# Pieces of an FFT placed by tables between the matmuls of an MLP, with the PSUM banks written down

## The chip, the cores and the metric

The kernel runs on one core of one Trainium2 chip. The metric is the device time of one execution in microseconds, and the kernel before has a median of 809.14 us over 3 runs (807.16 to 809.75). The engines are called as in the profile: PE (TensorE matmuls), PEld (TensorE weight loads), DVE (VectorE), ACT (ScalarE), POOL (GpSimd) and SP (SyncE, here only a queue that issues DMAs).

## What is computed

```python
X = np.fft.rfft(x, axis=1)                    # x: 8 batches, 3008 rows, 256 columns, float32
y = np.fft.irfft(X * (filt_r + 1j * filt_i)[None], n=3008, axis=1)
h = y.reshape(8 * 3008, 256) @ w_in           # 24064 x 2048
g = np.maximum(h, 0) + alpha * np.minimum(h, 0)
out = g @ w_out                               # 24064 x 256, float32
```

Each of the eight batches is filtered along its rows in the frequency domain; all 24,064 filtered rows then go through a two-layer MLP with a leaky activation.

## The kernel before

**The MLP.** The loop at the end (L489 to L500) walks over 48 blocks of 512 or 384 filtered rows, and each block has 16 **steps**, 768 in all. A step does `up(j)` for the present block: two matmuls at L414 into a PSUM tile `hps`. In every odd step the pair of `hps` banks is full, and ACT copies it to SBUF (`gtb`, L420), after which DVE works the activation out in three instructions (two at L423, one at L424). The step also does `down` for the block before: three or four matmuls at L433 into `op`, which ACT copies out every eighth step (L438) and SP stores (L396, two or three DMAs each time). Two batches make twelve blocks, so 96 steps go by while one batch's rows pass. There are two `hps` buffers, two `op` buffers and three `osb` buffers.

**The FFT.** A batch of 3008 = 47 x 64 rows is transformed in four kinds of **pieces**, each of which takes one bank of a two-bank pool, `psF`:

- A (16 pieces, L158): one matmul (L164) on the rows `xs`, evicted by ACT to `asb`. After each four pieces SP saves `asb` to DRAM (`save_a`, L167), and when all four parts are there, SP reads them back turned into `at` with four DMAs of 384 KB (`turn_a`, L171). This is the first turned array.
- B (12, L180): two matmuls (L184) on `at`. Two DVE instructions read the bank (L188 to `ww`, L189 to `uu`), so that the bank is held until the second has ended. POOL then issues two DMAs that swap the halves of `ww` into `sw` (L191).
- S (12, L194): DVE adds `sw` to `uu`. It needs no bank.
- C (12, L199): two matmuls (L209) on `uu`, evicted by ACT to `v`. After each three pieces SP writes `v` to DRAM (`turn_c`, L212, four DMAs), and after the last three it waits for these writes and reads everything back into `zt` with four DMAs (L224). This is the second turned array.
- D (16, L226): four small matmuls (L231) on `zt`, evicted by ACT to `yT`, which the MLP's `up` reads.

`at`, `asb`, `v` and `zt` have one buffer each; `uu` has four, `ww` and `sw` three; `xs` has four, which POOL loads (L125) for the next batch.

**What sets the order.** The schedule is manual: every engine runs its instructions in the order in which the program issues them, and a plan (a dictionary from step to pieces, L442) says which pieces are issued ahead of `up` and `down` of which step. Batches 0 to 2 have plans of their own. For a batch b from 3 to 7, with p = 96 (b - 1), the plan before (L483 to L485 with L447 to L468) is regular, in steps counted from p:

| pieces | steps from p, before |
|---|---|
| A 0 to 15 | -68, then about every 2.4 steps, to -32; saves in the step of every fourth |
| `turn_a` | -27 |
| loads of the next batch's `xs` | 6, 10, 16, 20 |
| B 0 to 11 | 5, 9, 15, 19, 25, 29, 35, 39, 45, 49, 55, 59 |
| S | 8 steps behind its B |
| C | 12 steps behind its B; `turn_c` one step behind every third, the last with `zt` at 72 |
| D 0 to 15 | 91, 92, 93, 94, 95, then every second step to 117 |

Since 96 steps lie between two batches, B and C of a batch fall together with the A pieces of the next one and the D pieces of the one before. A piece that gets a bank whose earlier piece hasn't been evicted makes PE wait, and with it everything behind it in PE's order. The pool of two banks chooses the bank of each piece when the program is built. In the built program it takes the two banks in turn, but for 30 places out of 439 where one piece gets the bank of the piece just before it.

Of the kernel before, what the change touches and what calls it, by code (L numbers as in the profile page):

```python
# [11 lines left out]
FP32 = mybir.dt.float32  # L12
# [6 lines left out]
NB = 8  # L19
DFF = 2048  # L20
NH = 32
AF = mybir.ActivationFunctionType
OP = mybir.AluOpType

# [40 lines left out]
def kernel(  # L65
# [10 lines left out]
    nc = tc.nc  # L76
# [16 lines left out]
    p_osb = ctx.enter_context(tc.tile_pool(name="p_osb", bufs=3))  # L93
    psH = ctx.enter_context(tc.tile_pool(name="psH", bufs=2, space=bass.MemoryType.PSUM))
    psO = ctx.enter_context(tc.tile_pool(name="psO", bufs=2, space=bass.MemoryType.PSUM))
    psF = ctx.enter_context(tc.tile_pool(name="psF", bufs=2, space=bass.MemoryType.PSUM))
    dram = ctx.enter_context(tc.tile_pool(name="dram", bufs=1, space=bass.MemoryType.DRAM))
    a_dram = dram.tile([NB, 96, NH, D], FP16, name="a_dram")
    v_dram = dram.tile([NB, 96, NH, D], FP16, name="v_dram")
    ctx.enter_context(tc.manual_schedule())  # L100
# [20 lines left out]
    def xrow(b, h, c):  # L121
        return bass.AP(tensor=x.tensor, offset=x.offset + (b * NFFT + NH * h + 8 * c) * D,
                       ap=[[N2 * D, N1], [1, 8 * D]])

    def load_x(b, c):  # L125
        xs = p_x.tile([2 * N1, 8 * D], FP16, name="xs")
        for h in range(2):
            nc.gpsimd.dma_start(out=xs[h * N1 : h * N1 + N1], in_=xrow(b, h, c))  # L128
        return xs

    def load_filt(dst, pbase, src, ka, kb):
# [7 lines left out]
            in_=bass.AP(tensor=src.tensor, offset=src.offset + (N1 - ka) * D,  # L139
                        ap=[[47 * D, 32], [-D, n], [1, D]]))  # L140

    def bank(wide=False):
        if wide:
            return psH.tile([128, 2, 512], FP32, name="hps")[:, 0]
        return psF.tile([128, 512], FP32, name="psF")


    class Fft:
# [5 lines left out]
        def start_a(self):  # L154
            self.asb = p_fft.tile([96, NH, D], FP16, name="asb")
            self.at = p_fft.tile([128, NK1, D], FP16, name="at")

        def piece_a(self, i, evict, wide=False):  # L158
            if i == 0:
                self.start_a()  # L160
            xs = xc[(self.b, i // 4)]
            ps = bank(wide)
            o = (i % 4) * 512
            nc.tensor.matmul(ps[0:96], wf1_s, xs[:, o : o + 512], start=True, stop=True)  # L164
            evict(self.asb[:, 2 * i : 2 * i + 2].rearrange("p a d -> p (a d)"), ps[0:96])
# [5 lines left out]
        def turn_a(self, eng, ka=0, kb=NK1):  # L171
            for h in range(2):
                for c in range(2):
                    r = h * 48 + c * NK1
                    q = c * 64 + NH * h
                    eng.dma_start(
                        out=self.at[q : q + NH, ka:kb],
                        in_=a_dram[self.b, r + ka : r + kb].rearrange("k s d -> s k d"))

        def piece_b(self, kp):  # L180
            px = bank().rearrange("p (k d) -> p k d", k=2)
            for kh in range(2):
                k1 = 2 * kp + kh
                nc.tensor.matmul(px[:, kh], twf_s[:, k1], self.at[:, k1], start=True, stop=True)  # L184
            uu = p_uw.tile([128, 2, D], FP16, name="uu", bufs=4)
            ww = p_uw.tile([128, 2, D], FP16, name="ww")
            sw = p_uw.tile([128, 2, D], FP16, name="sw")
            nc.vector.tensor_mul(ww, px, filts_s[:, 2 * kp : 2 * kp + 2])  # L188
            nc.vector.tensor_mul(uu, px, filt_s[:, 2 * kp : 2 * kp + 2])  # L189
            for o in (0, 64):  # L190
                nc.gpsimd.dma_start(out=sw[o : o + 64], in_=ww[64 - o : 128 - o])  # L191
            self.uw[kp] = uu, sw
# [6 lines left out]
        def piece_c(self, kp, evict, pv=None):  # L199
            if kp == 0:  # L200
                self.v = p_fft.tile([128, NK1, D], FP16, name="v")
                self.zt = p_fft.tile([96, NH, D], FP16, name="zt")
            us = self.uw.pop(kp)
            if pv is None:
                pv = bank().rearrange("p (k d) -> p k d", k=2)
            for kh in range(2):
                k1 = 2 * kp + kh
                for u in us:
                    nc.tensor.matmul(pv[:, kh], twi_s[:, k1], u[:, kh], start=u is us[0], stop=u is us[-1])  # L209
            evict(self.v[:, 2 * kp : 2 * kp + 2], pv)  # L210
# [26 lines left out]
    def on_act(o, i):  # L237
        nc.scalar.activation(o, i, AF.Copy)  # L238

# [75 lines left out]
    xc = {(0, c): load_x(0, c) for c in range(4)}  # L315
# [88 lines left out]
    class Block:  # L404
# [4 lines left out]
        def up(self, j):  # L409
# [6 lines left out]
            if j % 2 == 1:  # L416
                g = gtb[:, turn[0] % 17]
                turn[0] += 1
                m = p_m.tile([128, 2, 512], FP16, name="m")
                nc.scalar.activation(g[:, :, 0:tn], self.hps[:, :, 0:tn], AF.Copy)  # L420
                for i in range(2):
# [5 lines left out]
        def down(self, q):  # L427
            n = self.tn // 128
            for w in range(n * q, n * (q + 1)):
# [5 lines left out]
                if k == 15 and (si % 2 == 1 or si == n - 1):  # L435
                    m = si % 2 + 1
                    osb = p_osb.tile([128, 2, D], FP32, name="osb")
                    nc.scalar.activation(osb[:, 0:m], self.op[:, 0:m], AF.Copy)  # L438
                    for lane in range(m):
# [4 lines left out]
    def put(step, fn, *args):  # L444
        plan.setdefault(step, []).append((fn, args))

    def plan_fft(b, a0, ga, ta, b0, gap, add, lag, d0, quarters, x_at):  # L447
        f = Fft(b)
        for i in range(16):
            put(int(a0 + ga * i), f.piece_a, i, on_act)  # L450
        for c in range(4):
            put(int(a0 + ga * (4 * c + 3)), f.save_a, c)
            if b + 1 < NB:
                put(x_at[c],
                    lambda b=b, c=c: xc.update({(b + 1, c): load_x(b + 1, c)}))
        for q in range(quarters):
            w = NK1 // quarters
            put(ta, f.turn_a, nc.sync, w * q, w * q + w)
        bs = [b0 + (2 * int(gap * kp / 2) if add else int(gap * kp)) for kp in range(12)]
        for kp in range(12):  # L460
            put(bs[kp], f.piece_b, kp)
            if add:
                put(bs[kp] + add, f.piece_s, kp)
            put(bs[kp] + lag, f.piece_c, kp, on_act)
        for q in range(4):
            put(bs[3 * q + 2] + lag + 1, f.turn_c, q)
        for i in range(16):
            put(d0 + min(i, 4) + 2 * max(i - 4, 0), f.piece_d, i, on_act)  # L468
# [13 lines left out]
    plan_fft(2, 66, 2, 97, 109, 4.5, 8, 12, 187, 4, (110, 114, 118, 122))  # L482
    for b in range(3, NB):  # L483
        p = 96 * (b - 1)
        plan_fft(b, p - 68, 2.4, p - 27, p + 5, 5, 8, 12, p + 91, 1, (p + 6, p + 10, p + 16, p + 20))  # L485

    prev = None
    step = 0
# [43 lines left out]
```

## Time and profile before

| | |
|---|---|
| time, median of 3 runs | 809.14 us (807.16 to 809.75) |
| span of the profiled execution, first to last instruction | 805.5 us |
| own time of the profiled execution | not given beside its span |
| first `up` of step 0 | 37.58 us into the span |
| granted TensorE clock, mean | 0.999 |
| busy: DVE, ACT, POOL | 647.0, 599.1, 140.4 us |
| moved by DMA | 100.59 MB, 125 GB/s on the mean |

Busy times of the profile are sums of the durations of instructions. A matmul's recorded duration holds its passage through the array, so that two matmuls in a row overlap in the record; what PE really gives is seen in the distance from one start to the next. "Idle before" of a group is the time in which its engine did nothing ahead of it, and the name behind the arrow is what ended the wait. All stretches are counted in us from the span's start.

### The profile page before, as it was taken

How to read it: one execution, taken by the hardware profiler on the slowest of the kernel's cores; microseconds unless marked ns; L12 is line 12 of the kernel's file. 1: busy time of each engine (PE TensorE's matmuls, PEld its weight loads, DVE VectorE, ACT ScalarE, POOL GpSimd, SP SyncE). 2: the span in 40 equal slices, each digit the busy share in tenths (PEclk: the TensorE clock that was granted, in tenths of full speed). 3: DMA queues.
4: the chain of work that ended last, by engine and by line, in shares of the span. 5: the costliest groups of instructions: out<-in, count | busy, mean ns of one | idle time of the engine just before them, and what ended most of it. 6: DMA issues, size and time to landing. Idle time of an engine off the chain costs nothing.

```text
span 805.5 us, 16163 instructions
## 1 busy us (share of the span) xinstructions
PE 781.5 (97%) x5980; PEld 538.6 (67%) x5980; DVE 647.0 (80%) x1449; ACT 599.1 (74%) x836; POOL 140.4 (17%) x269
## 2 busy tenths in 40 slices
PE   6999999999999999999999999999999999999997
PEld 5756666666666666766667666766666666776665
DVE  4797985899879897798878888798877999777773
ACT  3788677878778777877868877787877867696663
POOL 7410330232004220131102321032200222000000
PEclk9999999999999999999999999999999999999999
DMA  9977457674756446574484543854465233511111
GB/s 187 199 146 207 106 133 176 185 153 120 166 135 125 110 128 149 138 142 112 112 200 99 113 126 104 211 110 112 114 160 141 53 97 85 134 40 34 41 40 53
DMA packets 94247, 100.59 MB, mean 125 GB/s; under 512 B 11320, under 2 KB 81992, under 8 KB 94040
## 3 DMA queue, kind: packets, MB, share of 16 engines
q1 hardware_dynamic: 79512, 68.80, 32.3%
q0 software_dynamic: 14656, 30.75, 20.1%
q8 instruction: 47, 0.77, 0.4%
q14 instruction: 32, 0.26, 0.1%
HBM read 56.26 MB, written 46.66 MB: 128 GB/s over the span
## 4 chain that ended last, share of the span: by engine, by line
PE 74%; DVE 12%; ACT 7%; issue 3%; DMA 3%; SPq 1%; POOL 0%; ACTq 0%; DVEq 0%; POOLq 0%
PE op L433 32%; PE hps L414 31%; ACT gtb L420 4%; DVE m L423 4%; DVE gtb L424 3%; PE psF L209 3%; PE psF L164 2%; DVE ww L188 2%; DVE uu L189 2%; PE psF L231 2%; PE psF L184 1%; ACT asb L238 1%; DMA xs<-in_x_dram 1%; DMA v_dram<-v 1%; ACT osb L438 1%
## 5 line engine op out<-in xcount | busy, mean ns | idle before, releaser
L420 ACT ACTIVATE gtb<-hps 128x1024 f16<-128x1024 f32 (+1 forms) x384 | 385.4, 1004 | 111.2 <-PE hps L414 110.6
L433 PE MATMUL op<-wout_s,gtb 128*128 128x256 f16 x3008 | 451.1, 272 | 0.6 <-DVE gtb L424 0.6
L414 PE MATMUL hps<-yT,win_s 128*128 128x512 f16 (+1 forms) x1536 | 449.1, 374 | 0.4 <-ACT gtb L420 0.2
L433 PEld LDWEIGHTS <-gtb 128*128 128x128 f16 x3008 | 293.3, 98 | 189.5 <-DVE gtb L424 0.9
L423 DVE TENSOR_SCALAR m<-gtb,alm_s 128x512 f16<-128x512 f16 (+1 forms) x768 | 237.7, 351 | 108.1 <-ACT gtb L420 107.3
L424 DVE TENSOR_TENSOR gtb<-gtb,m 128x1024 f16<-128x1024 f16 (+1 forms) x384 | 261.6, 681 | 24.3 <-PE hps L414 0.5
L191 POOL DMA_DIRECT2D sw<-ww x168 | 87.7, 527 | 503.1 <-DVE ww L188 494.1
L414 PEld LDWEIGHTS <-win_s 128*128 128x128 f16 x1536 | 146.1, 98 | 31.1 <-issue 3.1
L238 ACT ACTIVATE yT<-psF 128x376 f16<-128x376 f32 x120 | 58.2, 485 | 25.4 <-PE psF L231 25.1
L238 ACT ACTIVATE asb<-psF 96x512 f16<-96x512 f32 x112 | 66.1, 591 | 12.4 <-PE psF L164 12.0
L238 ACT ACTIVATE v<-psF 128x512 f16<-128x512 f32 x84 | 50.2, 597 | 29.3 <-PE psF L209 28.9
L438 ACT ACTIVATE osb<-op 128x512 f32<-128x512 f32 x96 | 56.3, 586 | 6.1 <-issue 3.2
L188 DVE TENSOR_TENSOR ww<-psF,filts_s 128x512 f16<-128x512 f32 x84 | 57.4, 684 | 0.1
L189 DVE TENSOR_TENSOR uu<-psF,filt_s 128x512 f16<-128x512 f32 x84 | 57.2, 682 | 0.0
L164 PE MATMUL psF<-xs,wf_s 94*96 94x512 f16 x112 | 43.1, 385 | 1.7 <-ACT v L238 1.0
L231 PE MATMUL psF<-wi_s,zt 96*128 96x94 f16 x504 | 41.9, 204 | 2.5 <-DMA zt<-v_dram 1.6
L231 PEld LDWEIGHTS <-zt 96*128 96x128 f16 x512 | 35.4, 97 | 7.3 <-DMA zt<-v_dram 1.9
L128 POOL DMA_DIRECT2D xs<-in_x_dram x64 | 34.8, 555 | 25.6 <-PE psF L164 13.3
L209 PE MATMUL psF<-uu,twi_s 128*128 128x256 f16 x168 | 33.7, 274 | 4.9 <-DVE uu L189 4.5
L184 PE MATMUL psF<-at,twf_s 128*128 128x256 f16 x168 | 32.1, 272 | 0.2
L196 DVE TENSOR_TENSOR uu<-uu,sw 128x512 f16<-128x512 f16 x72 | 30.1, 418 | 0.0
L209 PEld LDWEIGHTS <-twi_s 128*128 128x128 f16 x192 | 16.7, 98 | 12.8 <-DVE uu L189 10.2
(57 smaller groups left out, 191.3 us busy)
## 6 DMA issues: line engine op xcount, KB each, us to landing
out_dram<-osb SPq DMA_DIRECT2D x128, 128.0 KB
xs<-in_x_dram POOLq DMA_DIRECT2D x64, 188.0 KB, 4.4
a_dram<-asb SPq DMA_DIRECT2D x28, 384.0 KB
sw<-ww POOLq DMA_DIRECT2D x168, 64.0 KB, 2.1
v_dram<-v SPq DMA_DIRECT2D x112, 96.0 KB
zt<-v_dram SPq DMA_DIRECT2D x28, 384.0 KB
at<-a_dram SPq DMA_DIRECT2D x20, 384.0 KB
at<-a_dram SPq DMA_DIRECT2D x32, 96.0 KB
```

The costliest lines, as they stand in the source:

```text
L188: nc.vector.tensor_mul(ww, px, filts_s[:, 2 * kp : 2 * kp + 2])
L189: nc.vector.tensor_mul(uu, px, filt_s[:, 2 * kp : 2 * kp + 2])
L191: nc.gpsimd.dma_start(out=sw[o : o + 64], in_=ww[64 - o : 128 - o])
L209: nc.tensor.matmul(pv[:, kh], twi_s[:, k1], u[:, kh], start=u is us[0], stop=u is us[-1])
L231: nc.tensor.matmul(ps[:, m], self.zt[:, 8 * g + 4 * mh + m, dh * 128 : dh * 128 + 128], wi3_s, start=True, stop=True)
L238: nc.scalar.activation(o, i, AF.Copy)
L414: nc.tensor.matmul(self.hps[:, j % 2, 0:tn], win_s[:, kt, j * 128 : (j + 1) * 128], yT[:, kt, self.t0 : self.t0 + tn], start=(kt == 0), st ...
L420: nc.scalar.activation(g[:, :, 0:tn], self.hps[:, :, 0:tn], AF.Copy)
L423: nc.vector.tensor_scalar(m[:, i, 0:tn], g[:, i, 0:tn], 0.0, a, OP.min, OP.mult)
L424: nc.vector.tensor_add(g[:, :, 0:tn], g[:, :, 0:tn], m[:, :, 0:tn])
L433: nc.tensor.matmul(self.op[:, si % 2], self.gts[k][:, 128 * si : 128 * si + 128], wout_s[:, k], start=(k == 0), stop=(k == 15))
L438: nc.scalar.activation(osb[:, 0:m], self.op[:, 0:m], AF.Copy)
```

## The change

The plan of batches 3 to 7 is replaced by five tables of steps, and the two banks of `psF` become two pools of one bank, with a string of 440 digits that says which of the two each piece takes, in the order of the calls. Of 439 neighbours in that string 50 have the same digit. The string also covers batches 0 to 2, whose plan is as before; its digits agree with what the pool chose up to step 70, and differ in part from there on.

In steps from p, the new plan of batches 4 to 7 is:

| pieces | steps from p, after |
|---|---|
| A 0 to 15 | -84, -82, -74, -69, -67, -61, -59, -58, -55, -53, -52, -50, -47, -44, -41, -40; saves one step behind every fourth |
| `turn_a` | -36 |
| loads of the next `xs` | 6, 10, 16, 20 |
| B | -22, -16, -12, 1, 7, 16, 23, 29, 38, 45, 51, 56 |
| S | -11, -4, -2, 11, 26, 32, 35, 41, 48, 52, 65, 67 |
| C | -1, 9, 20, 27, 34, 36, 42, 50, 54, 66, 70, 70; `turn_c` as before, the last with `zt` at 71 |
| D | 89, 90, 90, 92, 93, 94, 96, 99, 101, 101, 103, 110, 114, 121, 127, 129 |

Batch 3 keeps the old steps for A (with `turn_a` at -28), has its first three B at -12, -10 and -8 and its first S at -6, and follows the tables otherwise. The instructions themselves, their sizes and the number of DMAs are the same.

```diff
+BANKS = (
+    "010101010101010101010101010101001011100011011010100100100101010101010101010101010101010101010101"
...
+STEPS_A = (-84, -82, -74, -69, -67, -61, -59, -58, -55, -53, -52, -50, -47, -44, -41, -40)
+STEPS_B = (-22, -16, -12, 1, 7, 16, 23, 29, 38, 45, 51, 56)
+STEPS_S = (-11, -4, -2, 11, 26, 32, 35, 41, 48, 52, 65, 67)
+STEPS_C = (-1, 9, 20, 27, 34, 36, 42, 50, 54, 66, 70, 70)
+STEPS_D = (89, 90, 90, 92, 93, 94, 96, 99, 101, 101, 103, 110, 114, 121, 127, 129)
...
-    psF = ctx.enter_context(tc.tile_pool(name="psF", bufs=2, space=bass.MemoryType.PSUM))
+    psF = [ctx.enter_context(tc.tile_pool(name=f"psF{i}", bufs=1, space=bass.MemoryType.PSUM)) for i in range(2)]
...
+    order = iter(BANKS)
...
-        return psF.tile([128, 512], FP32, name="psF")
+        return psF[int(next(order))].tile([128, 512], FP32, name="psF")
...
-        plan_fft(b, p - 68, 2.4, p - 27, p + 5, 5, 8, 12, p + 91, 1, (p + 6, p + 10, p + 16, p + 20))
+        f = Fft(b)
+        steps_a = STEPS_A if b > 3 else [int(2.4 * i) - 68 for i in range(16)]
+        steps_b = STEPS_B if b > 3 else [max(st, 2 * kp - 12) for kp, st in enumerate(STEPS_B)]
+        for i in range(16):
+            put(p + steps_a[i], f.piece_a, i, on_act)
+            if i % 4 == 3:
+                put(p + steps_a[i] + 1, f.save_a, i // 4)
+        if b + 1 < NB:
+            for c in range(4):
+                put(p + (6, 10, 16, 20)[c], lambda b=b, c=c: xc.update({(b + 1, c): load_x(b + 1, c)}))
+        put(p + steps_a[15] + 4, f.turn_a, nc.sync)
+        for kp in range(12):
+            put(p + steps_b[kp], f.piece_b, kp)
+            put(p + max(STEPS_S[kp], steps_b[kp] + 6), f.piece_s, kp)
+            put(p + STEPS_C[kp], f.piece_c, kp, on_act)
+            if kp % 3 == 2:
+                put(p + STEPS_C[kp] + 1, f.turn_c, kp // 3)
+        for i in range(16):
+            put(p + STEPS_D[i], f.piece_d, i, on_act)
```

More of the change, by code (lines that the diff above doesn't have):

```diff
@@ L21 @@
 NH = 32
+BANKS = (
+    "010101010101010101010101010101001011100011011010100100100101010101010101010101010101010101010101"
+    "010101010101010101010010101010101010110101010011001011101010010101011001010101010101010110101011"
+    "001010110101010101010010010101010101010010101101010100110101010010101010101011011010101010101011"
+    "010100101010110010101011010101010101001001010101010101001010110101010011010101001010101010101101"
+    "10101010101010110101010101010101010101011010101010010101"
+)
+STEPS_A = (-84, -82, -74, -69, -67, -61, -59, -58, -55, -53, -52, -50, -47, -44, -41, -40)
[3 more added lines that the diff above has]
+STEPS_D = (89, 90, 90, 92, 93, 94, 96, 99, 101, 101, 103, 110, 114, 121, 127, 129)
 AF = mybir.ActivationFunctionType
```

## The prediction

> **What bounds the kernel now.** First the head of the page: span, busy shares, then the groups of the two MLP matmuls.
>
> ```profile
> span 805.5 us, 16163 instructions
> PE 781.5 (97%) x5980; PEld 538.6 (67%) x5980; DVE 647.0 (80%) x1449; ACT 599.1 (74%) x836; POOL 140.4 (17%) x269
> L433 PE MATMUL op<-wout_s,gtb 128*128 128x256 f16 x3008 | 451.1, 272 | 0.6 <-DVE gtb L424 0.6
> L414 PE MATMUL hps<-yT,win_s 128*128 128x512 f16 (+1 forms) x1536 | 449.1, 374 | 0.4 <-ACT gtb L420 0.2
> ```
>
> PE is the engine that is nearly always busy, and its two big groups hardly wait. But 451.1 + 449.1 is more than the span: recorded matmuls overlap, so 97% is no measure of what is left. What PE gives is read from starts, in the timeline of PE inside batch 4 (start, length, line):
>
> ```profile
> 355.36 0.60 PE L433 MATMUL op<-wout_s,gtb 128*128 128x256 f16 x4
> 355.80 0.38 PE L184 MATMUL psF<-at,twf_s 128*128 128x256 f16 x2
> 356.02 0.59 PE L414 MATMUL hps<-yT,win_s 128*128 128x512 f16 x2
> 356.45 0.60 PE L433 MATMUL op<-wout_s,gtb 128*128 128x256 f16 x4
> ...
> 357.75 0.38 PE L209 MATMUL psF<-uu,twi_s 128*128 128x256 f16 x2
> ...
> 358.84 0.38 PE L164 MATMUL psF<-xs,wf_s 94*96 94x512 f16 x1
> ...
> 359.93 0.38 PE L184 MATMUL psF<-at,twf_s 128*128 128x256 f16 x2
> ...
> 361.67 0.60 PE L433 MATMUL op<-wout_s,gtb 128*128 128x256 f16 x4
> 362.44 0.39 PE L209 MATMUL psF<-uu,twi_s 128*128 128x256 f16 x2 [0.18 <-DVE uu L189]
> ```
>
> Four `down` matmuls take 0.44 us from start to start (355.36 to 355.80), a B or C piece 0.22 (355.80 to 356.02), two `up` matmuls 0.43 (356.02 to 356.45). A step without pieces is 0.87 us, one with a piece about 1.09. At 361.67 the four `down` should have let C go at 362.11; it went at 362.44, 0.33 us late, though the idle time shown is only 0.18. What ended the wait is B's second eviction on DVE:
>
> ```profile
> 357.61 0.68 DVE L189 TENSOR_TENSOR uu<-psF,filt_s 128x512 f16<-128x512 f32 x1
> ...
> 360.50 0.69 DVE L424 TENSOR_TENSOR gtb<-gtb,m 128x1024 f16<-128x1024 f16 x1
> 361.10 0.68 DVE L188 TENSOR_TENSOR ww<-psF,filts_s 128x512 f16<-128x512 f32 x1
> 361.70 0.68 DVE L189 TENSOR_TENSOR uu<-psF,filt_s 128x512 f16<-128x512 f32 x1
> ```
>
> B went to PE at 359.93, and its bank came free at 361.70 + 0.68 = 362.38, after 2.45 us: the MLP's addition stands ahead of it on DVE. C takes that bank two steps behind B, after some 2.0 us. The B of 355.80 was free at 358.29; its bank went to the A of 358.84, three steps behind, which did not wait. So **two steps are too few and three are enough**. Now the waits of PE and of its weight loads from 236 to 648 us, which is from B of batch 3 to the last of these events (who waited for whom, us in total, times, longest):
>
> ```profile
> PE psF L209 <- DVE uu L189: 4.2, 14, 0.8
> PEld L209 <- DVE uu L189: 9.4, 22, 0.9
> PEld L164 <- DVE uu L189: 3.5, 12, 0.3
> ```
>
> The first row is the only one that this stretch has for PE, so nothing else holds it there. The loads give the count: 22 + 12 = 34 delays. In the built program, exactly 34 of the 60 B pieces of batches 3 to 7 are followed at two steps' distance by a piece in the same bank: eight a batch from 3 to 6, two in batch 7.
>
> **The change part by part.**
>
> *The 34 delays go.* With the new tables and digits the next user of a B's bank comes at two steps once, at three 4 times, and at four or more 55 times. The loads' idle time, 9.4 + 3.5 = 12.9 us, is the upper end. A load that isn't held up is done ahead, under a matmul of 0.11 us (0.44 / 4), so up to 34 x 0.11 = 3.7 us of it is no loss: the lower end is 9.2. Taking the delays singly from starts, as 0.33 above, gives 0.15 to 0.93 each, 10.3 in all, and that I take: **-10.3 us**. Nothing that PE did in these delays is lost, and what is late next is DVE and ACT, by two stretches of about 96 steps, in batches 4 and 6 (length, busy of PE, PEld, DVE, ACT, POOL):
>
> ```profile
> 332.00:428.00 96.00, 94.52 (x690) 63.45 (x689) 80.16 (x180) 75.01 (x105) 16.84 (x32) 1.00 0.56 131
> ...
> 523.00:619.00 96.00, 94.52 (x689) 63.43 (x688) 80.17 (x180) 75.00 (x105) 16.85 (x32) 1.00 0.55 131
> ```
>
> After 2.5 us less a batch, DVE has 80 us of work in 93, so it does not become the bound. The twelve B are also spread over 78 steps instead of 54.
>
> *Batches 1 and 2.* Their steps stay and the digits differ a little. One C (step 151) no longer takes the bank of the B two steps ahead, an A (step 72) now does; and in batch 3 one C (step 201) still does. With 0.4 gained and 0.1 + 0.3 lost, all sizes out of the 34, this is 0; ends -0.5 and +0.9.
>
> *Banks behind ACT.* In batches 3 to 7 a bank that ACT evicts is used again after one step 16 times, before never. Before, such cases stand in batches 1 and 2, and mostly cost nothing; the worst is the B below, one step behind an A in its bank. It should have started 0.11 us after the last C matmul and came after 0.39:
>
> ```profile
> 116.17 0.27 PE L209 MATMUL psF<-sw,twi_s 128*128 128x256 f16 x1
> 116.56 0.38 PE L184 MATMUL psF<-at,twf_s 128*128 128x256 f16 x2
> ```
>
> So 0 to 16 x 0.28 = 4.5 us. I take 0.3, since the densest new place, five pieces for ACT in steps p + 34 to 38, is 5 x 0.6 + 2 x 1.0 = 5.0 us of ACT (the pieces' and `gtb`'s mean durations, rows below) against 5 x 0.87 + 6 x 0.22 = 5.7 us of PE.
>
> ```profile
> L420 ACT ACTIVATE gtb<-hps 128x1024 f16<-128x1024 f32 (+1 forms) x384 | 385.4, 1004 | 111.2 <-PE hps L414 110.6
> L238 ACT ACTIVATE asb<-psF 96x512 f16<-96x512 f32 x112 | 66.1, 591 | 12.4 <-PE psF L164 12.0
> ```
>
> *The first turned array.* This is the step that loses its cover. From a batch's last A to its first B there were 37 steps; now there are 18, from p - 40 to p - 22: 18 x 0.87 and four C or B pieces at 0.22 are 16.5 us. The last A of batch 4 stands in PE's timeline, and SP's goes on from it (stores, save, turned read, stores, `v`, `zt`):
>
> ```profile
> 303.81 0.38 PE L164 MATMUL psF<-xs,wf_s 94*96 94x512 f16 x1
> ```
>
> ```profile
> 305.11 2.21 SPq L396 DMA_DIRECT2D out_dram<-osb  x3
> 307.42 0.38 SPq L169 DMA_DIRECT2D a_dram<-asb  x1
> 310.40 2.10 SPq L176 DMA_DIRECT2D at<-a_dram  x4
> 312.77 2.12 SPq L396 DMA_DIRECT2D out_dram<-osb  x2
> 314.93 2.11 SPq L218 DMA_DIRECT2D v_dram<-v  x4
> 321.13 1.72 SPq L224 DMA_DIRECT2D zt<-v_dram  x4
> ```
>
> The page's size of one of the four, and a stretch under them, with DMA share and GB/s at its end:
>
> ```profile
> at<-a_dram SPq DMA_DIRECT2D x20, 384.0 KB
> ```
>
> ```profile
> 313.00:316.00 3.00, 3.00 (x23) 2.02 (x22) 2.30 (x6) 1.96 (x2) 0.00 (x0) 1.00 1.19 221
> ```
>
> The turned read is issued 6.6 us behind the A; the three stores ahead of it stay there after the change, with the four writes of an earlier `turn_c` (2.1 us) ahead of these. Its 4 x 384 KB and the two stores, 1.8 MB, at the last row's 221 GB/s are an estimated 8.3 us, 8.8 with the slow start: in all 15.4 us of 16.5. So about 1 us is to spare in each of batches 4 to 7, and none if SP is a little later. I take 0.1 us a batch, 0.4 in all; ends 0 and 4 x 1.5 (the four writes in front with nothing hiding them, less the spare, and some contention). That the `zt` read now stands eleven steps behind the turned read, before three, gains nothing by itself: no row of PE waits for either in the stretch above.
>
> *The next x rows.* POOL loads them at p + 6, and the first A that needs them moves from p + 28 to p + 12. On POOL only the swaps of one B (now at p + 1) stand ahead. A B of PE with a load behind it as now, POOL's issues, and the page's medians from issue to landing:
>
> ```profile
> 335.70 0.38 PE L184 MATMUL psF<-at,twf_s 128*128 128x256 f16 x2
> ```
>
> ```profile
> 338.01 1.03 POOL L191 DMA_DIRECT2D sw<-ww  x2 [36.38 <-DVE ww L188]
> 339.03 1.05 POOL L128 DMA_DIRECT2D xs<-in_x_dram  x2
> ```
>
> ```profile
> xs<-in_x_dram POOLq DMA_DIRECT2D x64, 188.0 KB, 4.4
> ...
> sw<-ww POOLq DMA_DIRECT2D x168, 64.0 KB, 2.1
> ```
>
> That is 3.3 + 0.5 + 4.4 = 8.2 us behind the B, and eleven steps are 9.2 us or more, even in the short block, whose steps are 0.76 (0.43 x 384/512 + 0.44): 8.4 and some 0.8 for pieces. I take 0.2 us for a slow landing, ends 0 and 3.
>
> *What stays free.* S stands at least 6 steps, 5.2 us, behind its B, whose second swap is issued after 2.8 and lands in 2.1; if S waits, it holds DVE, which has room. Against D, `zt` loses one step of lead (18 instead of 19), and gains that SP no longer issues the turned read just ahead of it. The last C comes 3 steps behind its S instead of 4, of which the addition needs about two. Loads, saves and issues keep their number.
>
> **Sum.** -10.3 + 0 + 0.3 + 0.4 + 0.2 = -9.4 us, so the span goes from 805.5 to 796.1. The profile gives no own time beside its span; the runs' median, 809.14, lies 3.6 above it, and I leave that as it is: **799.7 us**.
>
> **The rivals.**
>
> *ACT's banks take over (partial gain).* If the 16 short reuses cost the full 0.28 us, 4.2 us come back: 804. For it: 50 neighbours share a bank instead of 30. Against it: 30 did so before without one PE wait for ACT in the stretch above. The Trainium skill's page "Perfetto Trace Analysis", section "Matmuls", speaks for this rival: independent groups should rotate through different banks, and the change rotates less; the trace's waits do not bear that out so far, because who evicts, and how late, decided.
>
> *The turned read comes too late (slower).* If it lands later than 16.5 us behind the last A, PE stands before B 0 in batches 4 to 7, in order, with nothing to pass it. It eats the gain at 9.4 / 4 = 2.4 us of lateness, and from 3.0 the kernel is slower by more than a measurement can tell. Were the read served at half the rate (110 GB/s, 16 us instead of 8.3), it would be late by 6.6: 4 x 6.6 - 9.8 = +17, 826 us. For it: the spare of only 1 us. Against it: the `v` writes and `zt` that competed move away.
>
> *Nothing comes of it.* PE is shown at 97%, and if that were its limit, or if DVE's lateness only moved to another wait, the time would stay at 809. Against it: the starts show 34 dated gaps, and DVE has a sixth of its time free. On the first half the Trainium skill, "Perfetto Trace Analysis", section "Identifying the Most-Contended Engine", says that matmul busy share is no good measure since matmuls overlap; the two MLP groups, 900 us in a span of 805.5, agree.
>
> **How the numbers follow.** Forecast, 797 to 802: 0.72. Short reuse or a late landing of about 1 us, 802 to 806.5: 0.16. Nothing: 0.05, at 806.7 to 811.6. Slower: 0.07. A measurement of this kernel tells about 0.3% (2.4 us) from no change. So faster 0.88, same 0.05, slower 0.07. The range is 796.5 to 804.5: below it lies only the loads' full idle time (12.9 instead of 10.3), above it the upper ends of two costs together.
>
> **What would show it.** Right: no wait of PE or its loads for `uu` L189 from batch 3 on but one, 96 steps in about 93 us where the stretches show 95 to 96, DVE and ACT as busy as before. Wrong: waits of PE for `at` or `xs` DMAs ahead of L184 or L164, waits for ACT's `asb`, `v` or `yT` ahead of `psF` matmuls, or of L433 for `gtb`.

## The result, and the profile after

The changed kernel takes **798.04 us** (median of 4 runs, 796.51 to 799.77), beside 808.15 us for the kernel before on the same chip (806.38 to 809.75, 4 runs). The ratio is 0.9879, with a 95% interval of 0.9858 to 0.9901: about 10 us faster, where 9.4 us were forecast. The profiled execution took 796.51 us itself, its span is 794.6 us, and its granted clock is 0.999 as before.

The head of the page after, with the groups of the two MLP matmuls, of `op` (L447, before L433), of C (L223, before L209) and of B (L198, before L184). The lines quoted here stand 14 lower in the kernel after than in the one before:

```profile
span 794.6 us, 16129 instructions
PE 776.0 (98%) x5980; PEld 540.0 (68%) x5980; DVE 645.2 (81%) x1449; ACT 596.8 (75%) x836; POOL 140.7 (18%) x269
PE 86%; DMA 6%; ACT 3%; DVE 2%; SPq 1%; issue 1%; POOL 0%; ACTq 0%; DVEq 0%; POOLq 0%
L447 PE MATMUL op<-wout_s,gtb 128*128 128x256 f16 x3008 | 451.1, 272 | 0.6 <-DVE gtb L438 0.6
L223 PE MATMUL psF<-uu,twi_s 128*128 128x256 f16 x168 | 32.6, 273 | 0.2
L198 PE MATMUL psF<-at,twf_s 128*128 128x256 f16 x168 | 32.1, 272 | 0.5 <-DMA at<-a_dram 0.5
```

The same 5980 matmuls run, and the busy times of DVE and ACT are within 3 us of before. The third row is the chain of work followed back from the last instruction, as shares of the span by engine. On the page of before, that row and the group of C read:

```profile
PE 74%; DVE 12%; ACT 7%; issue 3%; DMA 3%; SPq 1%; POOL 0%; ACTq 0%; DVEq 0%; POOLq 0%
L209 PE MATMUL psF<-uu,twi_s 128*128 128x256 f16 x168 | 33.7, 274 | 4.9 <-DVE uu L189 4.5
```

So DVE's share of that chain falls from 12% to 2%, and the wait of C for `uu` is gone.

Now all the waits of PE and of its weight loads after, from 236 to 760 us (who waited for whom, us in total, times, longest), in the place of the 34 of before:

```profile
PEld L198 <- issue: 1.0, 2, 0.5
PE psF L198 <- DMA at<-a_dram: 0.5, 2, 0.3
PEld L223 <- DVE uu L203: 0.2, 1, 0.2
```

One load still waits for `uu`, which is the C at step 201 that was named. The new row is the turned array `at`, twice. A stretch of 93 us after (length, busy of PE, PEld, DVE, ACT, POOL) holds as many matmuls as 96 us before (690 and 689 in the rows of the prediction):

```profile
410.00:503.00 93.00, 93.00 (x694) 64.23 (x693) 78.55 (x177) 73.51 (x103) 16.84 (x32) 1.00 0.56 135
```

For what follows, the span is cut at the first `up` matmul of every 96th step in PE's timeline. "Loop" is from the first `up` of step 0 to that of step 767. The stretch ahead of step 0, which the change does not touch, takes between 37.6 and 41.3 us in the profiled executions, so loops are compared and not spans. A delay "from starts" is, as in the prediction, the distance between two starts on PE less what it is where nothing waits.

| us | 0-95 | 96-191 | 192-287 | 288-383 | 384-479 | 480-575 | 576-671 | 672-767 | loop |
|---|---|---|---|---|---|---|---|---|---|
| before | 103.63 | 94.81 | 95.38 | 96.01 | 95.38 | 96.01 | 90.20 | 82.62 | 754.04 |
| after | 102.91 | 95.30 | 94.16 | 93.09 | 93.13 | 93.43 | 88.73 | 82.27 | 743.03 |
| C one step later | 103.82 | 94.80 | 93.78 | 93.75 | 93.78 | 93.75 | 89.68 | 82.62 | 745.99 |
| C one step earlier | 103.64 | 94.81 | 97.75 | 98.38 | 97.74 | 98.46 | 90.04 | 82.62 | 763.44 |
| tables, pool's banks | 103.84 | 96.39 | 94.04 | 93.31 | 93.13 | 93.37 | 88.74 | 82.27 | 745.09 |
| digits, old steps | 103.35 | 94.80 | 96.38 | 97.02 | 96.39 | 97.11 | 90.20 | 82.62 | 757.86 |
| turned read later | 103.96 | 100.19 | 99.47 | 97.55 | 97.98 | 97.35 | 88.74 | 82.27 | 767.51 |
| B 0 later | 103.89 | 95.30 | 93.73 | 93.09 | 93.13 | 93.09 | 88.73 | 82.28 | 743.23 |
| four edits | 104.78 | 97.12 | 93.73 | 93.09 | 93.13 | 93.09 | 88.74 | 82.27 | 745.94 |

The last seven rows are the experiments below. Each ratio that they give is to the kernel before.

### The profile page after: what moved, and what is told of

The parts are those of the page before. It is cut to its first block, busy times and chain, and to the rows that moved or that the text cites. A ratio compares the mean times of both kernels' runs of the same rounds, so it can differ in the third digit from the quotient of the medians.

```text
span 794.6 us, 16129 instructions
## 1 busy us (share of the span) xinstructions
PE 776.0 (98%) x5980; PEld 540.0 (68%) x5980; DVE 645.2 (81%) x1449; ACT 596.8 (75%) x836; POOL 140.7 (18%) x269
## 4 chain that ended last, share of the span: by engine, by line
PE 86%; DMA 6%; ACT 3%; DVE 2%; SPq 1%; issue 1%; POOL 0%; ACTq 0%; DVEq 0%; POOLq 0%
PE op L447 37%; PE hps L428 37%; PE psF L178 3%; PE psF L245 3%; PE psF L223 2%; PE psF L198 2%; ACT gtb L434 2%; DMA at<-a_dram 2%; DMA a_dram<-asb 1%; DMA filt_s<-in_filt_i_dram 1%; DMA xs<-in_x_dram 1%; ACT asb L252 1%; SPq L410 1%; PE hps L295 1%; PE psF L324 1%
## 5 line engine op out<-in xcount | busy, mean ns | idle before, releaser
L447 PE MATMUL op<-wout_s,gtb 128*128 128x256 f16 x3008 | 451.1, 272 | 0.6 <-DVE gtb L438 0.6
L447 PEld LDWEIGHTS <-gtb 128*128 128x128 f16 x3008 | 293.3, 98 | 189.5 <-DVE gtb L438 0.9
L245 PE MATMUL psF<-wi_s,zt 96*128 96x94 f16 x504 | 40.3, 204 | 1.9 <-DMA zt<-v_dram 1.1
L223 PE MATMUL psF<-uu,twi_s 128*128 128x256 f16 x168 | 32.6, 273 | 0.2
L198 PE MATMUL psF<-at,twf_s 128*128 128x256 f16 x168 | 32.1, 272 | 0.5 <-DMA at<-a_dram 0.5
L223 PEld LDWEIGHTS <-twi_s 128*128 128x128 f16 x192 | 18.4, 98 | 3.7 <-DMA sw<-ww 0.8
```

What stands on the lines that cost most here:

```text
L245: nc.tensor.matmul(ps[:, m], self.zt[:, 8 * g + 4 * mh + m, dh * 128 : dh * 128 + 128], wi3_s, start=True, stop=True)
L447: nc.tensor.matmul(self.op[:, si % 2], self.gts[k][:, 128 * si : 128 * si + 128], wout_s[:, k], start=(k == 0), stop=(k == 15))
```

## The experiments

The theory to test is that of the prediction: PE lost its time where a piece took the bank of a B, evicted late by DVE, two steps behind it, and distance is what cures that. The rivals are that the written banks do it, or that PE is at its limit anyway.

**C one step later, nothing else.** In the kernel before, C stands 13 steps behind its B:

```diff
-        plan_fft(b, p - 68, 2.4, p - 27, p + 5, 5, 8, 12, p + 91, 1, (p + 6, p + 10, p + 16, p + 20))
+        plan_fft(b, p - 68, 2.4, p - 27, p + 5, 5, 8, 13, p + 91, 1, (p + 6, p + 10, p + 16, p + 20))
```

> The plan of before with one number changed: C comes 13 steps behind its B instead of 12, so that the next user of a B's bank is never two steps behind it (42 times three, 18 times more, read from the built program). If the distance behind B is the whole cause, the 34 delays go and this lands beside the changed kernel: 8.5 to 10.3 us below before, 798 to 800. In the short blocks three steps may be too few, which would leave up to 1.5 us. If the gain needs the tables (B spread over 78 steps, reads held apart, digits), it stays within 3 us of before: 805 or more.

Measured: 799.45 us (799.18 to 801.03, 4 runs), ratio 0.9896, interval 0.9865 to 0.9927. One digit gives 8.05 of the 11.01 us that the loop gained. The waits of PE and of its weight loads from 236 to 760 us are these:

```profile
PEld L414 <- issue: 2.2, 4, 0.5
PE psF L164 <- ACT v L238: 1.6, 4, 0.4
PEld L209 <- DVE uu L189: 0.4, 2, 0.2
```

Of the waits for `uu`, two short ones of weight loads are left. What is new is four A pieces that wait for ACT. One of them, on PE and then on ACT:

```profile
378.99 0.38 PE L209 MATMUL psF<-uu,twi_s 128*128 128x256 f16 x2
...
380.08 0.38 PE L184 MATMUL psF<-at,twf_s 128*128 128x256 f16 x2
380.85 0.38 PE L164 MATMUL psF<-xs,wf_s 94*96 94x512 f16 x1 [0.39 <-ACT v L238]
```

```profile
378.81 1.01 ACT L420 ACTIVATE gtb<-hps 128x1024 f16<-128x1024 f32 x1
379.72 0.59 ACT L438 ACTIVATE osb<-op 128x512 f32<-128x512 f32 x1
380.20 0.60 ACT L238 ACTIVATE v<-psF 128x512 f16<-128x512 f32 x1
```

The C of 378.99 has its bank free only at 380.80, since `gtb` and the output copy `osb` stand ahead of `v` on ACT. The A, one step behind, should have come at 380.30 and comes 0.55 late; the four cost 2.2 us. So ACT too can hold a bank for 1.8 us; DVE held B's for 2.4.

**C one step earlier.** The same digit, 11 in place of 12:

> The plan of before with C 11 steps behind its B: 12 users of a B's bank come one step behind it and 22 two. A bank is held 2.3 to 2.9 us and a step is 0.9 to 1.1, so a distance of one costs about 1.4 us and a distance of two 0.3: 12 x 1.4 + 22 x 0.3 = 23 us of delays instead of 10.3, so about 13 us slower than before, 818 to 824. If the distance does not matter, the same as before.

Measured: 819.51 us (2 runs), ratio 1.0140, interval 1.0093 to 1.0188. The waits from 236 to 760 us:

```profile
PEld L164 <- DVE uu L189: 18.7, 24, 1.4
PE psF L164 <- DVE uu L189: 12.1, 12, 1.1
PEld L231 <- DVE uu L189: 4.6, 10, 1.1
PE psF L231 <- DVE uu L189: 1.5, 2, 0.8
```

The same engine waits for the same eviction, up to 1.4 us at a time: twelve B pieces are now followed at one step's distance and 22 at two. A cause that can be turned down by a step and up by a step is shown. The loop's last stretch, which has no B, is the same 82.62 in all three.

**The tables without the written banks.** The kernel after, with one pool of two banks:

```diff
-    psF = [ctx.enter_context(tc.tile_pool(name=f"psF{i}", bufs=1, space=bass.MemoryType.PSUM)) for i in range(2)]
+    psF = ctx.enter_context(tc.tile_pool(name="psF", bufs=2, space=bass.MemoryType.PSUM))
...
-        return psF[int(next(order))].tile([128, 512], FP32, name="psF")
+        return psF.tile([128, 512], FP32, name="psF")
```

> The changed kernel with the five tables of steps but the pool's own choice of banks (one pool of two banks, no digits). In the built program the distances behind B are nearly the same (two steps once, three 4 times, four or more 55 times), and 14 reuses come one step behind an eviction by ACT. Theory: the steps do it, the digits nothing: within 0.5 us of the changed kernel, 797.5 to 799. If the written digits carry a part, 800 or more.

Measured: 799.10 us (798.09 to 800.11, 4 runs), ratio 0.9890, interval 0.9853 to 0.9928; its interval overlaps that of the kernel after almost wholly. It lies 0.1 us above the 797.5 to 799 that were expected and below the 800 of the other theory, so the time alone settles nothing; the stretches do. From step 192 on the six stretches sum to 544.86 us, after to 544.81. There the digits do nothing. What they save lies in steps 96 to 191: 1.09 us, of which 0.70 is one D that takes a B's bank:

```profile
233.72 0.34 PE L245 MATMUL psF<-wi_s,zt 96*128 96x94 f16 x4 [0.53 <-DVE uu L203]
```

The 0.93 us more in steps 0 to 95 are longer waits for the DMAs of `sw` (+0.6) and `zt` (+0.3) of batch 1, which no bank decides and which differ from execution to execution.

**Written banks without the tables.** The kernel before with its own steps, two pools and a string chosen for these steps, so that 22 pieces instead of 34 come two steps behind a B, and 12 come one step behind an A, whose bank ACT evicts:

```diff
-    psF = ctx.enter_context(tc.tile_pool(name="psF", bufs=2, space=bass.MemoryType.PSUM))
+    psF = [ctx.enter_context(tc.tile_pool(name=f"psF{i}", bufs=1, space=bass.MemoryType.PSUM)) for i in range(2)]
...
-        return psF.tile([128, 512], FP32, name="psF")
+        return psF[int(next(order))].tile([128, 512], FP32, name="psF")
```

> The kernel before with its own steps; only the choice of the psF bank is written down, by digits chosen for these steps (two pools of one bank in place of one pool of two). A string cannot free every B bank at these steps: pieces that take their bank two steps behind a B fall from 34 to 22, 16 take it three steps behind, and 12 pieces newly take a bank one step behind an eviction by ACT. Theory one (the distance behind B is the cause, and it is the tables that make the distance): the 12 delays that go, at 0.30 each by the kernel before, are worth 3.6 us, less up to 12 x 0.1 for the ACT banks; so 803 to 806 beside 807.7, some 22 delays in the records ahead of matmuls of psF behind uu evictions. Theory two (the written banks are the change, the tables only go with them): 798 to 800. Theory three (digits bring nothing): 807 to 808.5.

Measured: **812.51 us** (811.41 to 814.28, 4 runs), ratio 1.0063, interval 1.0041 to 1.0085. All three expectations missed: it is slower than before. The waits from 236 to 760 us (C is L218 here, A L173, `asb` L247):

```profile
PEld L218 <- DVE uu L198: 8.2, 18, 1.0
PEld L218 <- issue: 6.8, 12, 0.7
PE psF L218 <- DVE uu L198: 3.7, 11, 0.9
PE psF L218 <- DVE m L432: 2.2, 4, 0.6
PE psF L218 <- ACT asb L247: 2.2, 4, 0.6
PEld L173 <- DVE uu L198: 1.1, 4, 0.3
```

There are 18 + 4 = 22 waits of loads for `uu`, as chosen, and 12 new ones put down to "issue". One of these twelve on PE and on ACT, and beside it one that cost little (the C of 268.26):

```profile
268.26 0.38 PE L218 MATMUL psF<-uu,twi_s 128*128 128x256 f16 x2
...
278.00 0.38 PE L173 MATMUL psF<-xs,wf_s 94*96 94x512 f16 x1
...
278.65 0.60 PE L442 MATMUL op<-wout_s,gtb 128*128 128x256 f16 x4
279.80 0.38 PE L218 MATMUL psF<-uu,twi_s 128*128 128x256 f16 x2 [0.55 <-ACT asb L247]
```

```profile
277.76 1.02 ACT L429 ACTIVATE gtb<-hps 128x1024 f16<-128x1024 f32 x1 [0.62 <-PE hps L423]
278.68 0.59 ACT L447 ACTIVATE osb<-op 128x512 f32<-128x512 f32 x1
279.16 0.59 ACT L247 ACTIVATE asb<-psF 96x512 f16<-96x512 f32 x1
...
267.63 0.58 ACT L247 ACTIVATE asb<-psF 96x512 f16<-96x512 f32 x1
```

The A of 278.00 has its bank free at 279.75, again behind `gtb` and `osb`; C should have come at 279.09 and comes 0.71 late. Where no `osb` stands ahead, as for the `asb` of 267.63, C came 0.23 late. Taken from starts, the three of a batch cost 0.72 + 0.72 + 0.23 us, 6.7 in four batches; the 22 behind a B cost 8.1, where the 34 of before cost 10.3, so that the string gained 2.2 there. So a bank is dear when the next piece comes before its evictor can be done, whichever engine that is, and at the old steps this choice of digits, made for the distance from B alone, loses. (The wait of 297.45, put down to `m` on DVE, is of this kind too: `asb` ended at 297.39.)

**The turned read four steps later.** The spare of the first turned array was the thinnest number of the forecast, so this takes it away:

```diff
-        put(p + steps_a[15] + 4, f.turn_a, nc.sync)
+        put(p + steps_a[15] + 8, f.turn_a, nc.sync)
```

> The changed kernel with the turned read four steps later in the program, which puts it behind two or three stores on SP that wait for ACT. In the changed kernel's trace the turned read lands between 0.43 us too late and 0.26 us early in batches 4 to 7. Theory: no lead is left, so the delay shows in full: the read is issued some 4.5 us later, B 0 waits that long in four batches, 16 to 20 us slower than the changed kernel, 814 to 818. If there is still cover, less than 4 us.

Measured: 823.23 us (2 runs), ratio 1.0186, interval 1.0138 to 1.0235: 25 us slower than after, where 16 to 20 were expected. Two things were missed. Batch 3 waits as well, since its read also falls behind three stores on SP, so there are five waits and not four (from 222 to 760 us):

```profile
PE psF L198 <- DMA at<-a_dram: 15.6, 5, 3.9
```

And the matmuls behind each wait run at half pace. PE's timeline around the first of them, and two stretches (the number behind POOL's busy time is the granted clock):

```profile
227.42 0.60 PE L447 MATMUL op<-wout_s,gtb 128*128 128x256 f16 x4
231.07 0.38 PE L198 MATMUL psF<-at,twf_s 128*128 128x256 f16 x2 [3.06 <-DMA at<-a_dram]
...
232.49 1.06 PE L428 MATMUL hps<-yT,win_s 128*128 128x512 f16 x2
233.34 1.06 PE L447 MATMUL op<-wout_s,gtb 128*128 128x256 f16 x4
```

```profile
225.00:228.70 3.70, 3.02 (x22) 1.88 (x20) 2.65 (x7) 2.70 (x4) 0.00 (x0) 1.00 1.22 219
228.70:235.00 6.30, 3.92 (x17) 2.34 (x18) 2.92 (x7) 1.02 (x1) 1.04 (x2) 0.75 0.63 160
```

From starts, the five waits lose 3.22, 4.06, 2.77, 3.44 and 2.91 us, 16.4 in all, and what follows each loses 1.4 to 1.7 more, 7.8 in all. That makes up the 24.5 us by which this loop is longer than after (0.8 of the waits for `at` were there already, and steps 0 to 95 add 1.0).

**B 0 two steps later.** The other way round, room for the turned read:

```diff
-STEPS_B = (-22, -16, -12, 1, 7, 16, 23, 29, 38, 45, 51, 56)
+STEPS_B = (-20, -16, -12, 1, 7, 16, 23, 29, 38, 45, 51, 56)
```

> The kernel after with the first B piece of batches 4 to 7 two steps later (step -20 in place of -22 from the batch's origin; its S piece goes by the larger of -11 and the B step plus 6, so it stays). Nothing else is moved; the digits are the same. Theory (B0 stands at the edge of the turned read, whose spare is 0.0 plus or minus 0.4): the delays of 0.43 and 0.35 us ahead of B0 in batches 4 and 7 are gone, no matmul of psF by at waits for a DMA, the last up of the loop comes 0.8 us sooner: 797.2 beside 798.0. Rival (the wait is not the landing but the B piece's own start, or the steps behind it become late instead): the delays move to the S or C piece of the same batch, and the time stays at 798.0. The time alone cannot tell 0.1% apart; the records ahead of B0 can.

Measured: 798.26 us (797.07 to 800.18, 4 runs), ratio 0.9882, interval 0.9861 to 0.9904; the times cannot tell it from after. The records can. From 236 to 760 us the single wait left is

```profile
PEld L223 <- DVE uu L203: 0.2, 1, 0.2
```

In the table, steps 192 to 287 and 480 to 575 are shorter than after by 0.43 and 0.34 us, the delays of batches 4 and 7, and the other stretches from 96 on agree to 0.01. The theory holds; the gain is eaten by steps 0 to 95 in that execution (+0.98 us, among it a longer wait for `zt` of batch 1), which the edit does not touch.

**Four edits together.** B 0 as above, the A pieces of batches 2 and 3 a step later, and a new string of digits for these steps:

```diff
-    plan_fft(2, 66, 2, 97, 109, 4.5, 8, 12, 187, 4, (110, 114, 118, 122))
+    plan_fft(2, 67, 2, 98, 109, 4.5, 8, 12, 187, 4, (110, 114, 118, 122))
...
-        steps_a = STEPS_A if b > 3 else [int(2.4 * i) - 68 for i in range(16)]
+        steps_a = STEPS_A if b > 3 else [int(2.4 * i) - 67 for i in range(16)]
```

> The kernel after with four edits: the first B piece of batches 4 to 7 at -20; the A pieces of batch 2 and of batch 3 one step later each (and batch 2's turned read with them), so that those at steps 70 and 157 no longer share a step with a C piece; and the digits chosen anew for these steps, with no piece two steps behind a B and none in the same step as an ACT eviction of its bank. Theory (what is left in the kernel after is: 0.78 for at, 0.42 and 0.63 for A pieces in batches 2 and 3, 0.26 for the one C, 0.2 each at three more): 2.0 to 2.7 us go, 795.5 to 796.5 beside 798.0, and only the start, the wait for zt of batch 1 and the tail keep delays above 0.3. Rival (matmuls set the pace and the delays that are left hide behind one another): 797.5 to 798.5.

Measured: 800.07 us (799.32 to 801.54, 4 runs), ratio 0.9904, interval 0.9888 to 0.9921. It missed. From step 192 on it is as good as the kernel with B 0 later, but steps 0 to 191 lose 3.7 us against after. Against what was expected of the string, three A pieces still share step and bank with a C (from starts 0.63 each), one D waits 0.70 behind a B, and the C at step 129 waits 0.69 for a B's bank, where it waits 0.22 in after:

```profile
171.50 0.38 PE L198 MATMUL psF<-at,twf_s 128*128 128x256 f16 x2
...
174.36 0.39 PE L223 MATMUL psF<-uu,twi_s 128*128 128x256 f16 x2 [0.52 <-DVE uu L203]
```

So nothing that was run beats the kernel after by more than its times can tell.

## Why the prediction was right, step by step

The forecast was 799.7 us and a span of 796.1; measured were 798.04 and 794.6. The loop went down by 11.01 us, and the forecast's terms are found again in it, taken from starts on PE:

| term | forecast | measured |
|---|---|---|
| the 34 delays behind B | -10.3 | -10.3, all gone |
| batches 1 and 2, and the C at step 201 | 0 | -0.8 |
| banks one step behind ACT | +0.3 | 0 |
| turned array `at` | +0.4 | +0.8 |
| next `xs` rows | +0.2 | 0 |
| not counted: gaps under 60 ns | | -0.7 |
| sum | -9.4 | -11.0 |

*The 34 delays.* "Two steps are too few and three are enough" held: one step more in the old plan takes the waits for `uu` away, one step less makes them longer. All 34 are gone. The value from starts was a little short, since it took the delayed matmul alone. In the trace of before the next one is late too, by 0.010 us behind each of the 22 C and by 0.034 behind each of the 12 A, 0.6 us in all. This is most of the row of gaps under 60 ns, so the delays were worth 10.9 us. The upper end, the loads' idle time of 12.9, was not reached.

*Batches 1 and 2.* The figure is what is left of steps 0 to 191 (-0.23, in which after has 0.85 us of matmuls more, since three B and a C of batch 3 were moved there) and +0.26 for the C at step 201. Of it, 0.57 is the wait for `zt` of batch 1, 1.80 before and 1.23 after. That wait was 1.54, 2.04 and 2.35 in three of the experiments, so it is chance and no gain of the change. The same holds for the wait for `sw` of batch 1 (0.92 before, 0.76 after, 0.64 to 1.36 in the experiments). Without the two about -0.1 is left, so the forecast of 0 held, and 0.7 of the 11.0 us is luck.

*Banks behind ACT.* None of the 16 shows a wait, so the forecast of nearly nothing was right, but the bound of 0.28 us each was not: with `osb` ahead on ACT such a reuse costs 0.72, in the experiment with the digits alone. The trace of before had shown such a price already: at steps 70 and 157 an A in the step of a C takes its bank and comes 0.67 and 0.63 late, waiting for `v`. The five-in-five-steps sum was the wrong test; what the runs point to is whether `gtb` and `osb` both stand ahead of the eviction. In the built programs that is so where the bank's first user comes in the step right behind an `osb` copy: 4 of 17 such reuses with C one step later (0.55 each, the others at most 0.07), 8 of the 12 with the digits alone (0.72, the others 0.23), and none of the 16 in the kernel after. So the forecast of nearly nothing came out for another reason than the one it gave. The rival of "ACT's banks" was therefore nearer than its price said: 12 of them took more than the gain of the digits. The rotation rule cited there (the Trainium skill, "Perfetto Trace Analysis", section "Matmuls"), counted as neighbours in the same bank, is not borne out here: the changed kernel rotates less (50 such neighbours instead of 30) and waits less, and what agrees with the runs is the distance from the eviction's end.

*The turned array.* This is the step that was mis-sized. "About 1 us to spare" was none: SP around the last A of batch 4, and the B that it leads to,

```profile
292.68 1.81 SPq L232 DMA_DIRECT2D v_dram<-v  x4
294.90 2.40 SPq L410 DMA_DIRECT2D out_dram<-osb  x3
297.40 0.52 SPq L183 DMA_DIRECT2D a_dram<-asb  x1
301.65 2.33 SPq L190 DMA_DIRECT2D at<-a_dram  x4
304.08 3.31 SPq L410 DMA_DIRECT2D out_dram<-osb  x3
308.16 3.07 SPq L232 DMA_DIRECT2D v_dram<-v  x4
```

```profile
293.77 0.38 PE L178 MATMUL psF<-xs,wf_s 94*96 94x512 f16 x1
...
309.84 0.60 PE L447 MATMUL op<-wout_s,gtb 128*128 128x256 f16 x4
310.71 0.38 PE L198 MATMUL psF<-at,twf_s 128*128 128x256 f16 x2 [0.27 <-DMA at<-a_dram]
```

The turned read is issued 7.9 us behind the A, not 6.6. The A's own part is as before (3.6 us to the save), but from the save to the read, which waits for the save to land, are 4.25 us where the same row of before gave 2.98; in batches 5 to 7 it is 3.8 to 3.9. The read itself ends 8.9 us after its issue, as estimated (8.8). The forecast had read batch 4 of before alone, which is the shortest of the five there, both from save to read (2.98 to 3.45) and from the read's issue to its landing (8.8 to 9.8); from the last A to the landing the five take 14.9 to 16.5 us, so the spread of before had already used up the spare. In batches 4 to 7 of after it is 16.3 to 16.8. So B 0 waited in batches 4 and 7 (0.43 and 0.35 us from starts) and passed by 0.1 to 0.3 us in batches 5 and 6. The save now runs in front of a different stretch of SP's queue, with four `v` writes issued 4.7 us ahead of it; that these slowed it is argued from the rows and was not tried alone.

*The reads held apart.* In both kernels `zt` is issued after the turned read has landed and only when the `v` writes have, and no PE row from batch 3 on waits for it. So this part gains nothing, as the prediction put it, and the move of the turned read has only made its cover thin.

*The rivals.* "Nothing comes of it" is refuted. "The turned read comes too late" was priced by lateness alone. The run with the read four steps later gives the real price: on each wait of 2.8 to 4.1 us, the lost clock adds 1.4 to 1.7.

*The range.* Its ends, 796.5 and 804.5, are not what the prediction says of them: the loads' full idle time alone gives 797.1, which lies inside, and the upper end of the turned read alone (4 x 1.5 instead of 0.4) gives 805.3, which lies above. The time measured lies inside either way.

## What to carry to other kernels

A PSUM bank costs PE time if its next user comes sooner than the end of the eviction, so count from the matmul to the eviction's end, with all that stands ahead of it on its engine (here 2.4 us on DVE, 1.8 on ACT with two copies ahead), and turn it into steps. Move the steps first, since one step of distance gave 8 of 11 us, while the string of banks gave at most 1, or a loss on its own. When a plan moves an array's producer and its consumer closer, measure the whole way of the array in the trace (save, landing, read) and leave more room than its best case.

## What was not expected of the hardware

After PE had waited 2.8 to 4.1 us in the run with the later turned read, the granted clock fell (0.75 on the mean from 228.70 to 235.00), and matmuls took twice their time for some 3 us: four `down` and two `up` of 0.43 to 0.44 us each took 0.85 (232.49 to 233.34, and 233.34 to 234.19). Waits of up to 2.35 us, the longest for `zt` of batch 1 (in the run with four edits, clock 1.00 behind it), did not do that. The Trainium skill's page "TensorE: Matmul & The Clock Gate", section "Why this matters for your kernels", asks for no idle gaps above about 3 us between bursts of matmuls; the trace agrees, and shows it for a wait of 2.77 us too.
